# The opening of a chunked linear attention: own terms, diagonals and masks of two units by halves of heads, four head copies on another engine, and a later place for the loads of v

## Chip, cores and metric

The kernel runs on one core of one Trainium2 chip. The metric is the device time of one execution in microseconds (us). The engines are named as in the profile: PE is TensorE (matmuls, with PEld for its weight loads), DVE is VectorE, ACT is ScalarE, POOL is GpSimd, and SP is the queue that issues most DMA loads.

## What is computed

The reference chains two blocks. The first is a linear attention with a decaying state: 4 batches, 8 heads, 768 positions, 48 numbers a head.

```python
for t in range(S):
    kt, vt, rt = (k[:, :, t], v[:, :, t], r[:, :, t])
    cur = np.einsum('bhd,bhe->bhde', u[None] * kt, vt)
    y[:, :, t] = np.einsum('bhd,bhde->bhe', rt, state + cur)
    state = w[None, :, :, None] * state + np.einsum('bhd,bhe->bhde', kt, vt)
```

So a position sees its own key and value through `u` (the own term), and all earlier ones through powers of the decay `w`. The second block takes the 3072 rows of y (384 wide), scores them against 8 experts, gives each expert its 384 rows in the order of the scores, and runs each expert's two matrices (384 to 1024, a ReLU, 1024 to 384) over its rows. The change touches only the start of the first block.

## The kernel before

The attention is cut into 24 units, each 128 positions of one batch (`units`: for each of the 6 chunks in time, the 4 batches). For a unit, k and r are turned (heads in pairs, transposed on PE), and each is scaled by a table of powers of w, so that one matmul per head, `pairs`, gives all products of a key with a later position. Entries on and below the diagonal of that 128 x 128 square are not wanted. The diagonal is to hold the own term r·(u k). This is put together so:

- `own` (L439) multiplies r by k and by u on POOL, two instructions of 384 columns into `rk`. `own_sum` (L446) sums it over the 48 numbers of each head on DVE into `dd` (8 numbers a row).
- `diagonal` (L487) makes, for each of the 8 heads, a 128 x 128 square with `dd` on its diagonal, on ACT (L495), in the tile `AT`.
- `pairs` (L497) runs 16 matmul instructions into `g_ps` (L504), and then copies the products over `AT` where a mask allows it, in two DVE instructions (L508), one for each z, the place of a head in its pair.
- `outputs` (L531) multiplies v by `AT` on PE (L542), and ACT copies the result out (`x`, L560). `rows` turns it back (`x_ps`, L591), ACT copies it (`xr`, L598), and SP stores it.
- `keep` adds the unit to its batch's state, from keys scaled on POOL (`keys`, L433, tile `kss`, with the table `wk`).

There is one more step: eight heads are laid out so that the pairs need one head twice. `again_one` (L342) copies that head's 48 columns on ACT, once for k and once for r; the last of the four transposes of a unit's k or r reads the copy, and so does `keys`.

The decay tables come from `start` (L346): powers of w are formed on DVE in steps (`powers`, L378 to L387), then their reciprocal (L393), and two outer products `Q` (L395), one on POOL and one on DVE. ACT copies pieces of `Q` into the tables `WK` and `WR` (`table`, L420); unit 0 is scaled by the pieces of `Q` itself. `wk_turned` and `wk_table` give `wk` from `WK`, through PE. `spread_u` brings u to all 128 partitions with a matmul, and `copy_u` (L412) copies it to `u_bc` on ACT. `idle` (L415) issues transposes whose result nobody reads.

The order of the work is written out by hand: under `manual_schedule` each engine executes its instructions in the order in which `run` (L613) issues them. `run` opens with units 0 and 1 and the sums and diagonals for both, then loops over the units; iteration n turns unit n + 2, makes its diagonals, runs the pairs of unit n + 1, and finishes unit n. In the opening, unit 2's sum stands before unit 1's pairs and masks (L659 to L664). SP issues the loads in the order written at L357, and then three in each iteration: k and r of unit n + 5 and v of unit n + 4. There are 5 buffers for k and r, 6 for v, so k of unit 5 needs every reader of k of unit 0 to be done. The tiles `g_ps` and `y_ps` have one buffer each.

Of the kernel before, what the change touches and what calls it, by code (L numbers as in the profile page):

```python
# [10 lines left out]
F32 = mybir.dt.float32  # L11
# [5 lines left out]
ALU = mybir.AluOpType  # L17
AX = mybir.AxisListType
# [3 lines left out]
T = 128  # L22
# [252 lines left out]
class Mild:  # L275
# [65 lines left out]

    def again_one(self, n, x):  # L342
        t, HP, H, D = self.krs[:, n % self.NK, x], self.HP, self.H, self.D
        self.nc.scalar.copy(t[:, H, 0:D], t[:, HP, 0:D])

    def start(self):  # L346
# [3 lines left out]
        with nc.allow_non_contiguous_dma(reason="a row to the partitions"):  # L350
            for eng, z, aa, hh in ((nc.sync, 0, slice(0, half), slice(0, HP, 2)),
# [4 lines left out]
                eng.dma_start(self.wp[z * PD:z * PD + D, aa], self.w[hh].rearrange("h d -> d h"))  # L356
        for n, what in ((0, "kr"), (1, "kr"), (0, "v"), (2, "kr"), (1, "v"), (3, "kr"), (2, "v"), (4, "kr"), (3, "v")):  # L357
            self.load(n, what)
# [34 lines left out]
        nc.vector.reciprocal(AB[:, 1], AB[:, 0])  # L393
        for x, eng in ((0, nc.gpsimd), (1, nc.vector)):
            eng.tensor_mul(self.Q[:, x], AB[:, x, :, 1, :].unsqueeze(3).to_broadcast([128, HP, 9, 8]),  # L395
                           AB[:, x, :, 0, 0:8].unsqueeze(2).to_broadcast([128, HP, 9, 8]))
        Q = self.Q.rearrange("p x a i j -> p x a (i j)")
# [40 lines left out]

    def own(self, n):  # L439
        nc, H, D = self.nc, self.H, self.D  # L440
        rk = self.pool.tile([128, H, D], F32, name="rk")
        nc.gpsimd.tensor_mul(rk, self.krs[:, n % self.NK, 1, 0:H, 0:D], self.krs[:, n % self.NK, 0, 0:H, 0:D])  # L442
        nc.gpsimd.tensor_mul(rk, rk, self.u_bc)  # L443
        self.live[n].update(rk=rk)

    def own_sum(self, n):  # L446
        dd = self.pool.tile([128, self.H], F32, name="dd")
        self.nc.vector.tensor_reduce(out=dd, in_=self.live[n]["rk"], axis=AX.X, op=ALU.add)  # L448
        self.live[n]["dd"] = dd

# [35 lines left out]

    def diagonal(self, n, zs=(0, 1)):  # L487
        nc, HP = self.nc, self.HP
        if "AT" not in self.live[n]:
            self.live[n]["AT"] = self.pool.tile([128, 2, HP, T], F32, name="AT", bufs=3)  # L490
        AT, dd = self.live[n]["AT"], self.live[n]["dd"]
        for z in zs:
            for a in range(HP):
                h = self.head(a, z)
                nc.scalar.mul(AT[:, z, a, :], self.ident, dd[:, h:h + 1])  # L495

    def pairs(self, n, between=None):  # L497
        nc, HP, D = self.nc, self.HP, self.D
        kT, rT, AT = (self.live[n][x] for x in ("kT", "rT", "AT"))
        g_ps = self.ps.tile([128, 2, HP, T], F32, name="g_ps")  # L500
        for a in range(HP):
            for z in range(2):
                rows = slice(z * PD, z * PD + D)
                nc.tensor.matmul(g_ps[:, z, a, :], kT[rows, a, :], rT[rows, a, :], start=True, stop=True)  # L504
        if between is not None:
            between()
        for z in range(2):
            nc.vector.copy_predicated(out=AT[:, z], mask=self.mask.unsqueeze(1).to_broadcast([128, HP, T]),  # L508
                                      data=g_ps[:, z])

    def keep(self, n):
# [101 lines left out]
    def run(self, step):  # L613
        N, B, C, walk = self.N, self.B, self.C, self.walk
        self.live = {n: {} for n in range(N)}
        self.start()
        u_ps = self.spread_u()
        self.again_one(0, 0)
        k0 = self.keys_turned(0, True)
        self.again_one(0, 1)  # L620
        self.idle(2, "g_ps")
        r0 = self.r_turned(0)
        self.copy_u(u_ps)
        self.own(0)
        self.scaled(0, "k", k0, "pieces")
        self.scaled(0, "r", r0, "pieces")
        self.table(self.WK, "k")
        self.again_one(1, 0)
        self.table(self.WR, "r")
        self.again_one(1, 1)  # L630
        self.idle(2, "g_ps")
        k1 = self.keys_turned(1, True, walk.ps, "few")
        wk_ps = self.wk_turned()
        r1 = self.r_turned(1, walk.ps, "counts")
        self.wk_table(wk_ps)
        self.scaled(1, "k", k1, self.WK)
        self.own_sum(0)
        self.diagonal(0, (0,))
        self.again_one(2, 0)
        self.diagonal(0, (1,))  # L640
        self.again_one(2, 1)
        self.scaled(1, "r", r1, self.WR)
        self.own(1)
        self.keys(0)
        self.own_sum(1)
        nc, AB = self.nc, self.ones8
        nc.vector.tensor_mul(self.chunk, AB[:, 0, :, 1, 8], AB[:, 0, :, 1, 8])
        self.pairs(0)
        self.diagonal(1)
        self.own(2)  # L650
        chores = walk.constants()
        for n in range(N):
            self.load(n + 5, "kr")
            self.load(n + 4, "v")
            if n == 2:
# [3 lines left out]
            if n == 0:  # L659
                self.turn(2, True)  # L660
                self.own_sum(2)
                self.idle(3, "y_ps")
                self.pairs(1)
                self.keys(1)  # L664
# [1212 lines left out]
```

## Time and profile before

| | |
|---|---|
| median of 3 runs | 398.21 us (397.88 to 398.33) |
| the profiled execution | 398.63 us |
| its span, first to last instruction | 396.9 us |
| granted TensorE clock | 0.996 |
| PE busy in the span | 381.1 us (96%) |
| DVE | 267.4 us (67%) |
| ACT | 161.3 us (41%) |
| POOL | 137.9 us (35%) |
| the chain of work that ended last | PE 73%, DVE 10%, ACT 3%, POOL 3%, DMA 3% |

The span runs from the first to the last instruction of the profiled execution; its time holds 1.7 us more around it. Times of single instructions below are counted from the start of the span. The median comes from other executions of the same kernel. The attention with its gate fills the first 100 us or so, and the experts the rest. A row of a timeline gives the start, the duration (of a group: from its start to its end), the engine, the line, what is written and read, and how often; an idle time ahead of it is in brackets with what ended it. Neighbouring instructions on an engine overlap by some 0.1 us at their ends, so a sum over many of them is made from start to next start.

### The profile page before, as it was taken

Reading aid. Unit: us, or ns where it says so; the run is one execution under the profiler, and the core shown is the slowest. Engines: PE = TensorE matmul, PEld = TensorE weight load, DVE = VectorE, ACT = ScalarE, POOL = GpSimd, SP = SyncE. Lnnn points to the kernel's source line nnn. Section 1 sums busy time; section 2 is a strip of 40 time slices with the busy share of each in tenths; the row PEclk is TensorE's granted clock in tenths of the full one; section 3 lists DMA queues with packets and bytes.
Section 4 is the critical chain, followed back from the end, with each engine's and each line's share of the span. In section 5 each row is a group of like instructions: output and inputs, shape, how many; then the busy total and the mean of one; then the engine's idle time right before and its main releaser. Section 6 shows DMA issues by size and latency. Waiting matters only on the chain.

```text
span 396.9 us, 8692 instructions
## 1 busy us (share of the span) xinstructions
PE 381.1 (96%) x3243; PEld 289.4 (73%) x3243; DVE 267.4 (67%) x934; ACT 161.3 (41%) x429; POOL 137.9 (35%) x173
## 2 busy tenths in 40 slices
PE   7899999999999998999999999999999999999993
PEld 5678888888877764587578569558757857966981
DVE  6755777576885787967839819979578663952620
ACT  4997878888873311222222122221222222222220
POOL 7888877666732022031121120302303221040020
PEclk9999999999999999999999999999999999999998
DMA  9999999897692164641460650109209173370010
GB/s 121 158 184 205 197 201 171 151 177 153 125 327 81 42 247 169 215 164 40 152 246 12 220 208 2 60 0 334 84 21 359 57 281 120 99 300 2 2 61 26
DMA packets 95331, 57.29 MB, mean 144 GB/s; under 512 B 77232, under 2 KB 89520, under 8 KB 95280
## 3 DMA queue, kind: packets, MB, share of 16 engines
q1 hardware_dynamic: 91936, 47.21, 47.4%
q0 software_dynamic: 3104, 9.44, 6.7%
q8 instruction: 27, 0.44, 0.5%
q14 instruction: 24, 0.20, 0.2%
q10 hardware_dynamic: 240, 0.00, 0.0%
HBM read 47.20 MB, written 9.44 MB: 143 GB/s over the span
## 4 chain that ended last, share of the span: by engine, by line
PE 73%; DVE 10%; issue 4%; ACT 3%; POOL 3%; DMA 3%; SPq 1%; POOLq 0%; another core or an unknown queue 0%; DVEq 0%; ACTq 0%
PE h_ps L1539 26%; PE p_ps L1614 14%; PE o_ps L1641 7%; PE y_ps L542 6%; PE g_ps L504 4%; PE e_h_ps L1709 3%; PE kv_ps L521 2%; DMA krs<-in_k_dram 2%; PE kT_ps L458 2%; ACT AT L495 2%; PE x_ps L591 2%; PE lg_ps L571 2%; PE xT_ps L1526 2%; DVE W L1591 2%; PE rT_ps L458 1%
## 5 line engine op out<-in xcount | busy, mean ns | idle before, releaser
L1539 PE MATMUL h_ps<-xT,w 128*128 128x384 f32 (+1 forms) x384 | 120.8, 467 | 0.6 <-ACT e_o_sb L1721 0.6
L1539 PEld LDWEIGHTS h_ps<-xT,w 128*128 128x128 f32 x384 | 66.7, 190 | 39.1 <-issue 2.2
L1541 ACT ACTIVATE hid<-h_ps 128x384 f32<-128x384 f32 (+1 forms) x64 | 29.7, 464 | 91.3 <-PE h_ps L1539 79.9
L495 ACT ACTIVATE AT<-ident,dd 128x128 f32<-128x128 f32 x192 | 59.1, 391 | 2.0 <-DVE dd L448 1.8
L1511 POOL DMA_INDIRECT xg<-x_rows,tok x22 | 21.9, 997 | 88.0 <-issue 36.0
L1635 POOL DMA_INDIRECT out_dram<-o_all,to x16 | 17.6, 1103 | 99.2 <-DVE o_all L1623 66.8
L508 DVE COPY_PREDICATED AT<-mask,g_ps 128x512 f32<-128x512 uint8 x48 | 32.6, 732 | 12.1 <-PE g_ps L504 10.7
L1618 ACT COPY res<-p_ps 128x384 f32<-128x384 f32 (+2 forms) x28 | 13.2, 473 | 60.5 <-PE p_ps L1614 58.4
L1641 PE MATMUL o_ps<-w,hid 128*128 128x384 f32 x96 | 33.1, 488 | 0.0
L504 PE MATMUL g_ps<-rT,kT 48*128 48x128 f32 x384 | 27.9, 284 | 0.7 <-DVE AT L508 0.6
L436 POOL TENSOR_TENSOR kss<-krs,wk 128x384 f32<-128x384 f32 x24 | 24.3, 1017 | 8.0 <-DVE krs L340 5.5
L504 PEld LDWEIGHTS g_ps<-rT,kT 48*128 48x128 f32 x384 | 23.4, 187 | 4.0 <-PE unread_ps L418 0.5
L542 PE MATMUL y_ps<-AT,vts 128*64 128x128 f32 x384 | 25.7, 276 | 0.0
L443 POOL TENSOR_TENSOR rk<-rk,u_bc 128x384 f32<-128x384 f32 x24 | 24.2, 1007 | 1.9
L442 POOL TENSOR_TENSOR rk<-krs 128x384 f32<-128x384 f32 x24 | 24.6, 1024 | 0.2 <-DMA krs<-in_r_dram 0.2
L1641 PEld LDWEIGHTS o_ps<-w,hid 128*128 128x128 f32 x96 | 17.2, 190 | 9.5 <-issue 0.2
L542 PEld LDWEIGHTS y_ps<-AT,vts 128*64 128x64 f32 x384 | 20.6, 137 | 1.2 <-issue 0.7
L1614 PE MATMUL p_ps<-T,S 128*128 128x192 f32 x120 | 20.9, 328 | 0.0
L1591 DVE TENSOR_TENSOR H<-hid 128x512 f32<-128x512 f32 x12 | 7.9, 687 | 19.1 <-ACT hid L1541 19.1
L560 ACT COPY x<-y_ps 128x512 f32<-128x512 f32 x24 | 14.0, 585 | 14.6 <-PE y_ps L542 14.6
L1614 PEld LDWEIGHTS p_ps<-T,S 128*128 128x128 f32 x120 | 19.6, 190 | 0.1
L1614 PE MATMUL p_ps<-w,hid 128*128 128x192 f32 (+1 forms) x112 | 19.0, 316 | 0.0
(303 smaller groups left out, 684.9 us busy)
## 6 DMA issues: line engine op xcount, KB each, us to landing
w<-in_moe_w_dram SPq DMA_DIRECT2D x18, 1536.0 KB, 6.8
krs<-in_k_dram SPq DMA_DIRECT2D x24, 192.0 KB, 4.4
krs<-in_r_dram SPq DMA_DIRECT2D x24, 192.0 KB, 4.9
vts<-in_v_dram SPq DMA_DIRECT2D x24, 192.0 KB
x_rows<-xr SPq DMA_DIRECT2D x24, 192.0 KB, 3.0
xg<-x_rows,tok POOLq DMA_INDIRECT x22, 4.2
out_dram<-o_all,to POOLq DMA_INDIRECT x16, 2.7
out_dram<-o_sb,to POOLq DMA_INDIRECT x5
```

Source lines behind the costliest of these rows:

```text
L436: self.nc.gpsimd.tensor_mul(self.kss[:, n % self.NS].rearrange("p (g h) d -> p g h d", g=2)[:, :, :, 0:D], src, self.wk.rearrange("p (g h) ...
L442: nc.gpsimd.tensor_mul(rk, self.krs[:, n % self.NK, 1, 0:H, 0:D], self.krs[:, n % self.NK, 0, 0:H, 0:D])
L443: nc.gpsimd.tensor_mul(rk, rk, self.u_bc)
L495: nc.scalar.mul(AT[:, z, a, :], self.ident, dd[:, h:h + 1])
L504: nc.tensor.matmul(g_ps[:, z, a, :], kT[rows, a, :], rT[rows, a, :], start=True, stop=True)
L508: nc.vector.copy_predicated(out=AT[:, z], mask=self.mask.unsqueeze(1).to_broadcast([128, HP, T]), data=g_ps[:, z])
L542: nc.tensor.matmul(yv[q * PD:(q + 1) * PD, o // 2, o % 2, :], lhsT, rhs, start=(o // 2, q) not in seen, stop=stop, skip_group_check=True)
L1511: nc.gpsimd.indirect_dma_start(out=xg[:, c, :], out_offset=None, in_=x_dram[0:within, :], in_offset=bass.IndirectOffsetOnAxis(ap=tok[:, c: ...
L1539: nc.tensor.matmul(h_ps[:, 0:m], w1[:, f, ts(j, 128)], xT[:, f, 0:m], start=(f == 0), stop=(f == KD - 1))
L1541: nc.scalar.activation(hid[:, j, 0:m], h_ps[:, 0:m], AF.Relu)
L1614: nc.tensor.matmul(ps[:, q, :], left[a][:, j, :], right[b][:, j, :], start=(j == 0), stop=(j == KF // 2 - 1))
L1641: nc.tensor.matmul(o_ps, hid[:, j, ts(c, 128)], w2[:, j, :], start=(j == 0), stop=(j == KF - 1))
```

## The change

In `start`, both products `Q` are formed on DVE. The loads are reordered: v of each unit stands after k and r of a later unit, and the loop loads v of unit n + 3 instead of n + 4. The head copies of units 1 and 2 go from ACT to POOL. For units 0 and 1, `own` does its second product in two halves of heads, `own_sum` sums each half, `diagonal` makes each half, and the masks are two instructions by halves of the pairs, each over both z (`masked_half`), instead of one for each z. For unit 0, `own` begins with k times u. The order in `run` is new; in iteration 0, unit 2's sum now follows unit 1's pairs and masks.

```diff
--- before.py
+++ after.py
@@ -339,9 +339,9 @@
         kr, HP, H, D = self.krs[:, n % self.NK], self.HP, self.H, self.D
         self.nc.vector.tensor_copy(kr[:, :, H, 0:D], kr[:, :, HP, 0:D])
 
-    def again_one(self, n, x):
+    def again_one(self, n, x, copy=None):
         t, HP, H, D = self.krs[:, n % self.NK, x], self.HP, self.H, self.D
-        self.nc.scalar.copy(t[:, H, 0:D], t[:, HP, 0:D])
+        (copy or self.nc.scalar.copy)(t[:, H, 0:D], t[:, HP, 0:D])
 
     def start(self):
         nc, HP, H, D = self.nc, self.HP, self.H, self.D
@@ -354,7 +354,7 @@
                                    (nc.scalar, 1, slice(half, HP - 1), slice(HP + 2, HP + 3)),
                                    (nc.scalar, 1, slice(HP - 1, HP), slice(HP, HP + 1))):
                 eng.dma_start(self.wp[z * PD:z * PD + D, aa], self.w[hh].rearrange("h d -> d h"))
-        for n, what in ((0, "kr"), (1, "kr"), (0, "v"), (2, "kr"), (1, "v"), (3, "kr"), (2, "v"), (4, "kr"), (3, "v")):
+        for n, what in ((0, "kr"), (1, "kr"), (2, "kr"), (0, "v"), (3, "kr"), (1, "v"), (4, "kr"), (2, "v")):
             self.load(n, what)
         make_identity(nc, self.ident)
         nc.vector.memset(self.krs[:, :, :, :, D:PD], 0.0)
@@ -391,9 +391,9 @@
         for i in range(2):
             powers(i)
         nc.vector.reciprocal(AB[:, 1], AB[:, 0])
-        for x, eng in ((0, nc.gpsimd), (1, nc.vector)):
-            eng.tensor_mul(self.Q[:, x], AB[:, x, :, 1, :].unsqueeze(3).to_broadcast([128, HP, 9, 8]),
-                           AB[:, x, :, 0, 0:8].unsqueeze(2).to_broadcast([128, HP, 9, 8]))
+        for x in range(2):
+            nc.vector.tensor_mul(self.Q[:, x], AB[:, x, :, 1, :].unsqueeze(3).to_broadcast([128, HP, 9, 8]),
+                                 AB[:, x, :, 0, 0:8].unsqueeze(2).to_broadcast([128, HP, 9, 8]))
         Q = self.Q.rearrange("p x a i j -> p x a (i j)")
         M = PD
         self.pieces = {"k": ((slice(0, M + 1), Q[:, 0, :, M::-1]), (slice(M + 1, T), Q[:, 1, :, 1:T - M])),
@@ -436,17 +436,27 @@
         self.nc.gpsimd.tensor_mul(self.kss[:, n % self.NS].rearrange("p (g h) d -> p g h d", g=2)[:, :, :, 0:D], src,
                                   self.wk.rearrange("p (g h) d -> p g h d", g=2))
 
-    def own(self, n):
+    def own(self, n, u_first=False):
         nc, H, D = self.nc, self.H, self.D
+        k, r = (self.krs[:, n % self.NK, x, 0:H, 0:D] for x in range(2))
         rk = self.pool.tile([128, H, D], F32, name="rk")
-        nc.gpsimd.tensor_mul(rk, self.krs[:, n % self.NK, 1, 0:H, 0:D], self.krs[:, n % self.NK, 0, 0:H, 0:D])
-        nc.gpsimd.tensor_mul(rk, rk, self.u_bc)
+        if u_first:
+            nc.gpsimd.tensor_mul(rk, k, self.u_bc)
+        else:
+            nc.gpsimd.tensor_mul(rk, r, k)
+        for hs in self.parts(n):
+            nc.gpsimd.tensor_mul(rk[:, hs], rk[:, hs], r[:, hs] if u_first else self.u_bc[:, hs])
         self.live[n].update(rk=rk)
 
-    def own_sum(self, n):
-        dd = self.pool.tile([128, self.H], F32, name="dd")
-        self.nc.vector.tensor_reduce(out=dd, in_=self.live[n]["rk"], axis=AX.X, op=ALU.add)
-        self.live[n]["dd"] = dd
+    def parts(self, n):
+        H = self.H
+        return (slice(0, H // 2), slice(H // 2, H)) if n < 2 else (slice(0, H),)
+
+    def own_sum(self, n, part=0):
+        if "dd" not in self.live[n]:
+            self.live[n]["dd"] = self.pool.tile([128, self.H], F32, name="dd")
+        hs = self.parts(n)[part]
+        self.nc.vector.tensor_reduce(out=self.live[n]["dd"][:, hs], in_=self.live[n]["rk"][:, hs], axis=AX.X, op=ALU.add)
 
     def pair(self, t, a):
         s = 2 * a if t.shape[1] == self.H or 2 * a < self.HP else 2 * a + 1
@@ -484,7 +494,7 @@
         self.scaled(n, "k", kT_ps, self.WK if raw else None)
         self.scaled(n, "r", rT_ps, self.WR)
 
-    def diagonal(self, n, zs=(0, 1)):
+    def diagonal(self, n, zs=(0, 1), hs=range(99)):
         nc, HP = self.nc, self.HP
         if "AT" not in self.live[n]:
             self.live[n]["AT"] = self.pool.tile([128, 2, HP, T], F32, name="AT", bufs=3)
@@ -492,7 +502,8 @@
         for z in zs:
             for a in range(HP):
                 h = self.head(a, z)
-                nc.scalar.mul(AT[:, z, a, :], self.ident, dd[:, h:h + 1])
+                if h in hs:
+                    nc.scalar.mul(AT[:, z, a, :], self.ident, dd[:, h:h + 1])
 
     def pairs(self, n, between=None):
         nc, HP, D = self.nc, self.HP, self.D
@@ -504,9 +515,16 @@
                 nc.tensor.matmul(g_ps[:, z, a, :], kT[rows, a, :], rT[rows, a, :], start=True, stop=True)
         if between is not None:
             between()
-        for z in range(2):
+        for z in range(2) if n > 1 else ():
             nc.vector.copy_predicated(out=AT[:, z], mask=self.mask.unsqueeze(1).to_broadcast([128, HP, T]),
                                       data=g_ps[:, z])
+        return g_ps
+
+    def masked_half(self, n, g_ps, i):
+        half = self.HP // 2
+        at = slice(i * half, (i + 1) * half)
+        mask = self.mask.unsqueeze(1).unsqueeze(1).to_broadcast([128, 2, half, T])
+        self.nc.vector.copy_predicated(out=self.live[n]["AT"][:, :, at], mask=mask, data=g_ps[:, :, at])
 
     def keep(self, n):
         nc, HP, D, C = self.nc, self.HP, self.D, self.C
@@ -614,53 +632,61 @@
         N, B, C, walk = self.N, self.B, self.C, self.walk
         self.live = {n: {} for n in range(N)}
         self.start()
+        first, second = range(self.H // 2), range(self.H // 2, self.H)
+        nc, AB = self.nc, self.ones8
         u_ps = self.spread_u()
         self.again_one(0, 0)
         k0 = self.keys_turned(0, True)
+        self.copy_u(u_ps)
+        self.own(0, True)
         self.again_one(0, 1)
         self.idle(2, "g_ps")
         r0 = self.r_turned(0)
-        self.copy_u(u_ps)
-        self.own(0)
+        self.own_sum(0, 0)
         self.scaled(0, "k", k0, "pieces")
+        self.own_sum(0, 1)
         self.scaled(0, "r", r0, "pieces")
         self.table(self.WK, "k")
-        self.again_one(1, 0)
+        self.diagonal(0, hs=first)
         self.table(self.WR, "r")
-        self.again_one(1, 1)
-        self.idle(2, "g_ps")
+        self.diagonal(0, hs=second)
+        for x in range(2):
+            self.again_one(1, x, nc.gpsimd.tensor_copy)
+        self.idle(3, "g_ps")
         k1 = self.keys_turned(1, True, walk.ps, "few")
+        r1 = self.r_turned(1, walk.ps, "counts")
+        self.scaled(1, "k", k1, self.WK)
+        self.own(1)
+        self.scaled(1, "r", r1, self.WR)
+        g0 = self.pairs(0)
         wk_ps = self.wk_turned()
-        r1 = self.r_turned(1, walk.ps, "counts")
         self.wk_table(wk_ps)
-        self.scaled(1, "k", k1, self.WK)
-        self.own_sum(0)
-        self.diagonal(0, (0,))
-        self.again_one(2, 0)
-        self.diagonal(0, (1,))
-        self.again_one(2, 1)
-        self.scaled(1, "r", r1, self.WR)
-        self.own(1)
+        self.masked_half(0, g0, 0)
+        self.own_sum(1, 0)
+        self.diagonal(1, hs=first)
+        self.masked_half(0, g0, 1)
+        self.own_sum(1, 1)
+        self.diagonal(1, hs=second)
+        for x in range(2):
+            self.again_one(2, x, nc.gpsimd.tensor_copy)
         self.keys(0)
-        self.own_sum(1)
-        nc, AB = self.nc, self.ones8
+        self.own(2)
         nc.vector.tensor_mul(self.chunk, AB[:, 0, :, 1, 8], AB[:, 0, :, 1, 8])
-        self.pairs(0)
-        self.diagonal(1)
-        self.own(2)
         chores = walk.constants()
         for n in range(N):
             self.load(n + 5, "kr")
-            self.load(n + 4, "v")
+            self.load(n + 3, "v")
             if n == 2:
                 self.gate_weights()
             soon, split = n <= B, 0 < n < 3
             halves = ((0,), (1,)) if split else ((0, 1), ())
             if n == 0:
                 self.turn(2, True)
+                self.idle(3, "y_ps")
+                g1 = self.pairs(1)
+                for i in range(2):
+                    self.masked_half(1, g1, i)
                 self.own_sum(2)
-                self.idle(3, "y_ps")
-                self.pairs(1)
                 self.keys(1)
             else:
                 step(n, "first")
```

## The prediction

> **What bounds the kernel now.** I read the list of cores first (one core, 396.9 us, clock 0.996, so no clock effect), then the chain of waits over the first 70 us, then each engine's timeline from 4 to 31 us. The busy table by stage (columns: us, then PE, PEld, DVE, ACT, POOL busy with instruction counts, clock, DMA share, GB/s) shows where the opening ends:
>
> ```profile
> 10.00:15.00 5.00, 3.45 (x41) 2.61 (x39) 4.12 (x8) 4.97 (x18) 4.65 (x6) 1.00 1.51 163
> 20.00:25.00 5.00, 4.29 (x66) 3.73 (x62) 2.26 (x5) 5.00 (x17) 4.90 (x6) 1.00 1.27 178
> 25.00:30.00 5.00, 4.83 (x65) 4.10 (x66) 3.52 (x7) 5.00 (x18) 3.99 (x5) 1.00 1.14 194
> 40.00:50.00 10.00, 10.00 (x172) 8.68 (x168) 7.85 (x23) 8.63 (x25) 8.86 (x16) 1.00 1.03 195
> ```
>
> From 40 us TensorE is full; from 10 to 30 us ScalarE (ACT) is, and it paces TensorE. The chain of waits (start, us, what) agrees: VectorE (DVE) work leads to x_ps of unit 0, then it stays on ACT until 30.82, then on PE:
>
> ```profile
> 13.60 0.66 DVE kT L477
> 14.26 0.60 DVE rT L477
> 14.86 0.20 DVE dd L448
> ...
> 15.25 1.36 DVE AT L508 x2
> ...
> 18.92 0.40 PE x_ps L591 x4
> ...
> 19.34 0.48 ACT xr L598
> ...
> 30.23 0.60 ACT x L560
> 30.82 0.05 issue
> 30.87 0.60 PE x_ps L591 x4
> ```
>
> The ACT timeline shows which work this is. The last diagonals before the loop's copies are those of unit 2, from 15.35, just behind their sum dd of unit 2 (DVE 14.79 + 0.53 = 15.32):
>
> ```profile
> 12.70 2.45 ACT L495 ACTIVATE AT<-ident,dd 128x128 f32<-128x128 f32 x8
> 15.06 0.22 ACT L344 COPY krs<-krs 128x48 f32<-128x48 f32 x1
> 15.35 2.45 ACT L495 ACTIVATE AT<-ident,dd 128x128 f32<-128x128 f32 x8
> 17.71 0.21 ACT L344 COPY krs<-krs 128x48 f32<-128x48 f32 x1
> 17.83 0.58 ACT L560 COPY x<-y_ps 128x512 f32<-128x512 f32 x1
> 18.52 0.58 ACT L475 COPY kT<-kT_ps 112x512 f32<-112x512 f32 x1
> 19.34 0.48 ACT L598 COPY xr<-x_ps 128x384 f32<-128x384 f32 x1 [0.24 <-PE x_ps L591]
> ```
>
> From 15.35 to 30.8 ACT has about 0.35 us of gaps (18.41 to 18.52, 19.10 to 19.34). So what the change is worth is **when ACT starts the diagonals of unit 2**. That start carries through almost one to one, since what ACT does after it is unchanged and from 30.87 PE works back to back with its work fixed.
>
> **What the skill says.** (1) "PSUM — Partial Sum Buffer", Engine vs sequencer instructions: the ScalarE, VectorE and GpSimdE queues are strict FIFO. The trace agrees: each engine's rows stand in the order written. (2) "SBUF — State Buffer", Who interferes with whom: a VectorE instruction with two SBUF inputs and a GpSimd instruction that reads SBUF exclude each other, whichever starts second blocking until the first ends. The trace agrees:
>
> ```profile
> 11.39 1.01 POOL L436 TENSOR_TENSOR kss<-krs,wk 128x384 f32<-128x384 f32 x1
> 11.94 0.48 DVE L647 TENSOR_TENSOR chunk<-ones 128x4 f32<-128x4 f32 x1
> ```
>
> Chunk has the size of L384, which took 0.17; it took 0.48 and ended at 12.42, when GpSimd's product ended (12.40). (3) "GPSIMD Engine Reference", Performance versus the Vector engine: elementwise is about 2x slower on GpSimd. Here Q took 0.68 on GpSimd and 0.46 on DVE, 0.38 from its start to the next one's.
>
> **The change, part by part.** DVE steps below are from start to next start; all are from the timelines.
>
> *Copies of head blocks off ACT.* Four copies of L344 (0.23 each, 0.12 of ACT's time where the next follows): 4 x 0.12 = 0.5 us off ACT, before unit 2's diagonals. On GpSimd no such copy was seen: at least the 128x1 memset's 0.10, at most the 128x128 cast's 0.29; I take 0.13. They lie ahead of unit 1's and unit 2's own terms on GpSimd, 0.5 us in all (0.4 to 1.2; no gain, since GpSimd did none before).
>
> *Own term of unit 0, k by u first.* The copy of u on ACT moves ahead of the second head copy: u_ps is done near 5.46, so u is copied 5.5 to 5.97 and the first product runs 6.02 to 7.03, instead of starting at 7.05. Its halves (192 columns, 0.51 by L527) end near 7.66 and 8.13. Work for 0.9 us earlier, but its first product now lies over the powers on DVE. L382 is at 5.94, L387 at 6.14, both SBUF by SBUF. GpSimd gets in between: **L387 blocks from 6.14 to about 7.05, 0.9 us**. Bounds: 0, if the product starts after 6.14, and 1.0, the whole product. I take 0.9 (reciprocal at 7.25 instead of 6.36).
>
> *Q all on DVE.* One Q more, 0.38, on the engine. The first wants to start at 7.88, with GpSimd's second half going until 8.13: it waits 0.25; the second ends its turn at 8.88. Tables and unit 0's scaling wait for that, where before scaling began at 7.37.
>
> *The DVE order to the sum of unit 2.* From 8.88: half sum of unit 0 0.26 (0.46 less 192 columns at about 1 ns), k scaled 0.67, half sum 0.26, r scaled 0.67, unit 1 k 0.63, r 0.63 (before: 0.66), half mask 0.66 (512 elements, as one z of L508), half sum 0.28, half mask 0.66, half sum 0.28, chunk 0.30 (0.12 alone, 0.5 blocked), unit 2 k 0.60, r 0.60, both half masks of unit 1 1.32, then the sum of unit 2, 0.53. Neither half is in the trace: a half sum lies between half of L448's 0.46 and all of it, a half mask between 0.60 and 0.75 (L508 lasts 0.71 to 0.76), so four masks and four sums make −0.4 to +1.1. The list is 8.35, so it ends at 17.23 and unit 2's diagonals start near 17.28. **The sum now stands behind unit 1's masks**, whereas before it stood ahead of them (14.79 against 15.25). This is the one new wait on ACT. Queued behind it are the copies of y, kT and x of the loop; PE waits for these at x_ps.
>
> *What lies beside it.* ACT: Q 8.88, WK to 9.3, half diagonals 1.2, WR 0.7, half 1.2 (to 12.4), wk table after pairs(0) and its transposes near 12.55 to 13.0, unit 1's diagonals in two halves to 15.45, one copy, then idle until 17.28. GpSimd: keys of unit 0 wait for wk (13.05 to 14.05), own term of unit 2 to 16.1, which is 0.6 before DVE reaches its sum (16.7), so it and the four copies are hidden; if that cover is gone they add what passes 0.6. PE: one idle transpose more (0.19) inside the wait for k of unit 1 until 7.66; pairs(0) 10.8 to 11.9, wk's transposes, now behind it, to 12.5; pairs(1) 13.65 to 14.8, outputs of unit 0 to 15.9, all ahead of need.
>
> *Loads.* k and r of units 2 to 4 move up one place in SP's queue, about 1.19 us each (7.17 less 5.98): unit 2's transposes could start at 10.1 instead of 11.29. They feed a VectorE that isn't there before 14.2, so nothing comes of it. v of unit 0 moves two places back: it lands near 12.5 (r of unit 2 landed at 12.48 in that place), before outputs at 14.8. In the loop v is loaded a unit later, with three units of 4.6 us to spare. k of unit 5 must wait for keys of unit 0 (14.05), with r and v behind it on SP; before, it was issued at 18.24, so this is hidden.
>
> *Sum.* Unit 2's diagonals start 17.28 − 15.35 = 1.93 later. Of the gaps behind, 1.51 us from the start of x of unit 0 to xr shrinks to 1.28 (30.23 to 31.51, where nothing else is late): −0.23. Net **+1.7 us**. Against the profiled execution: span 396.9 → 398.6, its time 398.63 → 400.3. That execution lies 0.4 above the median, so on the median 398.2 → **399.9**. What is late next: the DVE chain itself.
>
> **Rivals.** (a) *Order without the block.* The first product starts after 6.14 and blocks no power, only the first Q, until about 7.2: the second Q's turn ends near 7.95 instead of 8.88, diagonals near 16.35, +1.0 − 0.23 = +0.8: 399.0. For it: 0.1 us decides. Against: the u copy is ready at 5.5. (b) *Faster: DVE keeps up.* If the masks by halves, with the pair's port free, cost so much less that the sum of unit 2 ends before 15.3, ACT isn't starved. Its own list from 7.45 (0.7 + 1.2 + 0.7 + 1.2 + 0.45 + 2.4 + 0.1) ends at 14.2, and unit 2's diagonals start up to 1.1 earlier: 397.1. For it: ACT loses 0.5 us of copies and starts unit 0 earlier. Against: 8.35 us of listed DVE work would have to take 6.4. It decides at 15.3. (c) *Nothing reaches the end*: the later search and weight loads set it, 398.2. Against: the chain of waits is PE for 73% with no wait for a DMA after the opening. (d) *More blocks*: own terms and keys block chunk, or GpSimd's copies cost 0.29 and the own term of unit 2 arrives after 16.7; +3: 401.2.
>
> **Chances.** Forecast 0.50, (a) 0.20, (b) 0.12, (c) 0.10, (d) 0.08. A measurement of this kernel can tell about 0.2%, 0.8 us, from no change. Slower by more: the forecast, half of (a), (d): 0.68. Within: (c), half of (a): 0.20. Faster: 0.12. Range 398.3 to 400.8: it takes in (a), leaves out (b), most of (d), and part of (c), about 0.2.
>
> **What would show it.** Right: L387 lasting about 1 us near 6.1; unit 2's sum at about 16.7 behind two 512-element masks; ACT idle for over 1.5 us before its diagonals; PE's gapless work from 32.5 instead of 30.87. Wrong: L387 at 0.18; unit 2's diagonals starting before 15.4; gapless PE before 30.9; or an unchanged end with a late opening.

## The result and the profile after

| | before | changed |
|---|---|---|
| median of 7 runs | 398.23 us (397.88 to 398.46) | 399.56 us (399.43 to 401.1) |
| profiled execution | 398.63 us | 399.56 us |
| its span | 396.9 us | 397.8 us |

The changed kernel takes 1.0040 of the time before (95% interval 1.0031 to 1.0050). The medians lie 1.3 us apart; the ratio goes with the averages, which are 1.6 us apart because two of the changed kernel's runs took 400.1 and 401.1 us.

The chain of waits of the changed kernel's trace holds only its last 15 us, so the opening is read from the timelines. First ScalarE, the same stretch as before the change (start, duration, engine, line, tiles, and in brackets the idle time ahead and what ended it):

```profile
12.71 2.45 ACT L506 ACTIVATE AT<-ident,dd 128x128 f32<-128x128 f32 x8
15.06 0.21 ACT L344 COPY krs<-krs 128x48 f32<-128x48 f32 x1
16.82 2.45 ACT L506 ACTIVATE AT<-ident,dd 128x128 f32<-128x128 f32 x8 [1.54 <-DVE dd L459]
19.17 0.21 ACT L344 COPY krs<-krs 128x48 f32<-128x48 f32 x1
19.29 0.58 ACT L578 COPY x<-y_ps 128x512 f32<-128x512 f32 x1
19.77 0.58 ACT L485 COPY kT<-kT_ps 112x512 f32<-112x512 f32 x1
20.56 0.48 ACT L616 COPY xr<-x_ps 128x384 f32<-128x384 f32 x1 [0.21 <-PE x_ps L609]
```

Unit 1's diagonals start when they did before, within 0.01 us, and ScalarE is free at 15.27. Then it waits 1.54 us for the sum of unit 2, so that unit 2's diagonals start at 16.82 instead of 15.35. Before, its longest wait in this stretch was one of 0.24 us. The VectorE timeline shows why the sum is late:

```profile
6.15 0.17 DVE L387 TENSOR_TENSOR ones<-ones 128x16 f32<-128x16 f32 x1
6.88 1.64 DVE L395 TENSOR_TENSOR Q<-ones 128x288 f32<-128x288 f32 x2
8.44 0.34 DVE L459 TENSOR_REDUCE dd<-rk 128x4 f32<-128x192 f32 x1
...
15.01 1.34 DVE L527 COPY_PREDICATED AT<-mask,g_ps 128x512 f32<-128x512 uint8 x2
16.25 0.54 DVE L459 TENSOR_REDUCE dd<-rk 128x8 f32<-128x384 f32 x1
```

Unit 1's two half masks (15.01) stand ahead of the sum (16.25); before, the sum started at 14.79, ahead of the masks. Earlier, the two Q take 1.64 us. The GpSimd timeline has the products that lie over them:

```profile
6.43 1.00 POOL L444 TENSOR_TENSOR rk<-krs,u_bc 128x384 f32<-128x384 f32 x1 [1.15 <-ACT u_bc L413]
7.51 1.46 POOL L448 TENSOR_TENSOR rk<-rk,krs 128x192 f32<-128x192 f32 x2
```

The delay then moves through PE unchanged. These are the starts of the transposes into x_ps at four places of the two traces (in both, the last of them comes after 128 us, so the attention lasts longer than the 100 us given above):

| x_ps | before | changed | later by |
|---|---|---|---|
| unit 0 | 18.75 | 19.92 | 1.17 |
| unit 3 | 30.87 | 32.08 | 1.21 |
| near 61 us | 61.27 | 62.48 | 1.21 |
| near 122 us | 122.01 | 123.22 | 1.21 |

Behind that 0.3 us is won back at the last matmuls of the gate (lg_ps), which start 0.83 us after x_ps of the unit ahead of them in the trace of before (125.62, 126.45) and 0.53 us after it in the changed one's (126.83, 127.36). Then the delay stays at 0.87 from the experts' first copy of hid at 159 us to about 270 us, and lies between 0.83 and 1.30 behind that. The last part differs from trace to trace (in the third experiment below, the copies of hid are 0.26 us behind before, then 0.44, then 0.8). The timed medians, 1.33 apart, are the better measure of the end.

### The profile page after: what moved, and what is told of

It is laid out like the page before. It is cut to its first block, busy times and chain, and to the rows that moved or that the text cites. A ratio compares the mean times of both kernels' runs of the same rounds, so it can differ in the third digit from the quotient of the medians.

```text
span 397.8 us, 8688 instructions
## 1 busy us (share of the span) xinstructions
PE 382.5 (96%) x3244; PEld 291.0 (73%) x3244; DVE 268.3 (67%) x937; ACT 160.8 (40%) x425; POOL 138.2 (35%) x178
## 5 line engine op out<-in xcount | busy, mean ns | idle before, releaser
L519 DVE COPY_PREDICATED AT<-mask,g_ps 128x512 f32<-128x512 uint8 x44 | 30.0, 733 | 12.5 <-PE g_ps L515 10.6
L448 POOL TENSOR_TENSOR rk<-rk,u_bc 128x384 f32<-128x384 f32 (+1 forms) x24 | 23.3, 972 | 1.8
L446 POOL TENSOR_TENSOR rk<-krs 128x384 f32<-128x384 f32 x23 | 23.2, 1010 | 0.0
```

The lines of the kernel that those rows point to most:

```text
L446: nc.gpsimd.tensor_mul(rk, r, k)
L448: nc.gpsimd.tensor_mul(rk[:, hs], rk[:, hs], r[:, hs] if u_first else self.u_bc[:, hs])
```

## Experiments

Each kernel was timed against the kernel before on its own chip, which there took 398.26 to 399.12 us. Ratios with their 95% intervals are therefore compared, not microseconds. For scale: 1 us is 0.0025. The last two columns come from each kernel's trace. "Theory 1" in the expectations is the explanation held at that point: the later sum on VectorE, the time lost in Q, and the own term of unit 2 on GpSimd all delay the start of unit 2's diagonals, and the end follows that start.

| kernel | ratio to before | unit 2's diagonals | xr of unit 0 |
|---|---|---|---|
| before | 1 | 15.35 | 19.34 |
| changed | 1.0040 (1.0031 to 1.0050) | 16.82 | 20.56 |
| order only | 1.0031 (1.0019 to 1.0043) | 17.22 | 20.96 |
| sum first | 1.0036 (1.0023 to 1.0049) | 16.55 | 20.50 |
| sum and own term first | 1.0012 (1.0004 to 1.0020) | 15.60 | 19.57 |
| Q alone | 1.0038 (1.0020 to 1.0056) | 16.57 | 20.48 |
| write only | 1.0028 (1.0018 to 1.0038) | 16.51 | 20.25 |
| product early | 1.0051 (1.0039 to 1.0063) | 16.88 | 20.62 |
| Q back | 1.0038 (1.0025 to 1.0051) | 17.42 | 21.16 |
| loads back | 1.0032 (1.0020 to 1.0044) | 16.82 | 20.56 |
| copies back | 1.0033 (1.0021 to 1.0045) | 16.85 | 20.59 |
| best parts | 1.0003 (0.9994 to 1.0011) | 15.52 | 19.50 |
| sum early | 0.9993 (0.9985 to 1.0001) | 15.10 | 19.07 |
| sum between | 0.9995 (0.9986 to 1.0003) | 14.70 | 19.19 |

The traces don't all have PE at the same pace in the opening (last section): before, Q alone, write only and sum between have the faster one, the others the slower. At the slower pace, unit 2's diagonals in the kernel before would start near 15.7 instead of 15.35. This is an estimate from the order-only trace, where ScalarE is through with unit 1's diagonals and the head copy behind them at about 15.57 + 0.12. So rows of unlike pace are compared only to some 0.35 us in the last two columns; the ratios do not depend on the traces.

**The order alone**, in the kernel before:

```diff
-                self.own_sum(2)
                 self.idle(3, "y_ps")
                 self.pairs(1)
+                self.own_sum(2)
```

> The kernel before with one edit: in iteration 0 the sum of unit 2 is issued behind unit 1's pairs and masks instead of ahead of them. Theory 1 (the order on VectorE alone is worth most of what the change lost): masks of unit 1 at 14.8, sum at 16.1, unit 2's diagonals near 16.65 instead of 15.35 on ScalarE, idle there for 1.4 us, xr of unit 0 near 20.4 instead of 19.34: slower than before by 1.1 us (0.8 to 1.4). Rival (masks ahead let PE and VectorE run ahead, so the wait is made good by unit 3): within 0.4 us of before.

It was 1.3 us slower. In its trace unit 0's sum and diagonals stand 0.6 us later than in the trace of before, for a reason given in the last section; within its own trace the cost of the order can still be seen, in the DVE timeline and then the ACT timeline:

```profile
14.45 0.69 DVE L477 TENSOR_TENSOR rT<-rT_ps,WR 112x512 f32<-112x512 f32 x1
15.39 1.36 DVE L508 COPY_PREDICATED AT<-mask,g_ps 128x512 f32<-128x512 uint8 x2 [0.25 <-PE g_ps L504]
16.65 0.54 DVE L448 TENSOR_REDUCE dd<-rk 128x8 f32<-128x384 f32 x1
```

```profile
17.22 2.45 ACT L495 ACTIVATE AT<-ident,dd 128x128 f32<-128x128 f32 x8 [1.44 <-DVE dd L448]
```

With the sum in its old place it would have followed the scaling, at about 14.45 + 0.60 = 15.05; it starts at 16.65, 1.6 us later, and ScalarE waits 1.44 us. So the order by itself costs most of what the whole change lost: about three quarters by the ratios (1.0031 of 1.0040), nearly all by the medians (1.30 of 1.33 us). The intervals overlap, so the share isn't known more closely. The rival, that the wait is made good by unit 3, fell.

**The sum first**, in the changed kernel: the same move undone.

```diff
                 self.turn(2, True)
+                self.own_sum(2)
                 self.idle(3, "y_ps")
...
                     self.masked_half(1, g1, i)
-                self.own_sum(2)
```

> The changed kernel with unit 2's sum moved back ahead of unit 1's pairs and masks, nothing else. Theory 1 (three causes close together: the order on VectorE, the time lost in Q, and GpSimd's own term of unit 2, which in the changed kernel ends only 0.3 us before VectorE reaches the sum): the sum now waits for GpSimd until 15.9, unit 2's diagonals start near 16.5 instead of 16.82, and unit 1's masks, now behind the waiting sum, end near 17.8, so xr of unit 0 stays within 0.3 us of 20.56 and the time is 399.3 to 399.7, no gain over the changed kernel. Rival (the order on VectorE alone made the change slow): diagonals of unit 2 at 15.5, xr near 19.5, time 398.3 to 398.5.

The ratio stays that of the changed kernel within the intervals, as theory 1 had it; undoing the order isn't enough. In the DVE timeline the sum now waits for GpSimd instead, and the masks behind it are late (16.43 instead of 15.01):

```profile
15.96 0.55 DVE L459 TENSOR_REDUCE dd<-rk 128x8 f32<-128x384 f32 x1 [0.86 <-POOL rk L448]
16.43 1.33 DVE L527 COPY_PREDICATED AT<-mask,g_ps 128x512 f32<-128x512 uint8 x2
```

**The sum and the own term first**: the same, and on GpSimd

```diff
-        self.keys(0)
         self.own(2)
+        self.keys(0)
```

> As the run before, and on GpSimd the own term of unit 2 stands ahead of the keys of unit 0, which wait for the table wk from ScalarE. Theory 1: the own term ends near 14.0, the sum of unit 2 follows the scaling at 15.0, diagonals of unit 2 start near 15.6, xr of unit 0 near 19.5, time about 1.0 us less than the changed kernel's, 398.3 to 398.7. If the lost time in Q were what the end follows, moving the sum would leave the diagonals of unit 2 past 16.4 and the time above 399.2.

1.0012: some 1.1 us of the 1.6 (1.0040 on 399.0) are back. Unit 2's diagonals start at 15.60 and xr of unit 0 at 19.57, both as expected:

```profile
15.60 2.45 ACT L506 ACTIVATE AT<-ident,dd 128x128 f32<-128x128 f32 x8 [0.31 <-DVE dd L459]
```

The order on GpSimd is not a part of the change: the kernel before has keys of unit 0 ahead of the own term of unit 2 as well. What the change moved is the table wk, which these keys read. Its transposes on PE now stand behind unit 0's pairs, and its copy on ScalarE behind unit 0's diagonals. Two rows of before (the copy, and the second product of the own term), then the changed kernel's:

```profile
8.99 0.47 ACT L431 COPY wk<-wk_ps 128x384 f32<-128x384 f32 x1
13.69 1.00 POOL L443 TENSOR_TENSOR rk<-rk,u_bc 128x384 f32<-128x384 f32 x1
```

```profile
12.29 0.48 ACT L431 COPY wk<-wk_ps 128x384 f32<-128x384 f32 x1 [0.38 <-PE wk_ps L427]
12.85 1.02 POOL L436 TENSOR_TENSOR kss<-krs,wk 128x384 f32<-128x384 f32 x1 [1.04 <-ACT wk L431]
14.91 1.01 POOL L448 TENSOR_TENSOR rk<-rk,u_bc 128x384 f32<-128x384 f32 x1
```

The copy of wk comes 3.3 us later, keys of unit 0 wait for it, and the own term of unit 2 ends at 15.92 instead of 14.69. This run goes round that delay; it doesn't undo it. So two things together hold about 70% of the loss by the ratios: the sum behind the masks, and the late wk ahead of unit 2's own term. With the first undone, the second kept unit 2's diagonals late (the run before). That undoing the second alone would gain nothing is read from the changed kernel's trace, where the own term is done 0.33 us before VectorE reaches the sum; it was not run. What is left, 1.0012, is not taken apart.

**Q alone**, in the kernel before:

```diff
-        for x, eng in ((0, nc.gpsimd), (1, nc.vector)):
+        for x, eng in ((0, nc.vector), (1, nc.vector)):
```

> The kernel before with one edit: both Q are formed on VectorE. Theory 1 (GpSimd, free of its Q, starts r by k when r of unit 0 lands at 6.45, and excludes the two Q in turn): the pair of Q takes 1.6 to 2.3 us from the start of the first to the end of the second, unit 0's scaling starts at 8.5 to 9.2 instead of 7.37, diagonals of unit 0 start 1.0 to 1.7 us later and the time is 0.8 to 1.5 us above before. Rival (VectorE only has one more product of 0.38 to do): Q takes 0.84, scaling starts at 7.75, and the time is within 0.4 us of before.

Its DVE timeline, and then GpSimd's:

```profile
6.88 2.19 DVE L395 TENSOR_TENSOR Q<-ones 128x288 f32<-128x288 f32 x2
8.99 0.74 DVE L473 TENSOR_TENSOR kT<-kT_ps,Q 112x260 f32<-112x260 f32 x2
```

```profile
6.58 1.00 POOL L442 TENSOR_TENSOR rk<-krs 128x384 f32<-128x384 f32 x1 [1.30 <-DMA krs<-in_r_dram]
7.67 1.09 POOL L443 TENSOR_TENSOR rk<-rk,u_bc 128x384 f32<-128x384 f32 x1
```

The pair takes 2.19 us where two alone take 0.76 (next run), each behind one of GpSimd's products; unit 0's diagonals start at 11.49 instead of 10.03 (both traces have the faster pace). The medians are 0.9 us apart, within what was expected; the ratio makes it 1.5 us (0.8 to 2.2). Either of two edits alone, the order or Q, thus costs the kernel before most of what the whole change does. The costs don't add: both delay the same start.

**Write only**: the changed kernel with GpSimd's first product exchanged.

```diff
-            nc.gpsimd.tensor_mul(rk, k, self.u_bc)
+            nc.gpsimd.tensor_copy(rk[:, 0:1, 0:1], self.u_bc[:, 0:1, 0:1])
+            for _ in range(2):
+                nc.gpsimd.memset(rk, 0.01)
```

> The changed kernel with GpSimd's first product of unit 0 (k by u, reading SBUF for 1.0 us) replaced by a one-column copy and two memsets of the same tile, which only write, for about 0.9 us in all; so unit 0's own term leaves out k and u. Theory 1 (a VectorE product with two SBUF inputs and a GpSimd instruction that reads SBUF exclude each other): the two Q take about 0.8 us from the start of the first instead of 1.64, less what GpSimd's half products still block; the first half sum starts at 7.8 to 8.1 instead of 8.44, unit 2's diagonals 0.3 to 0.6 us earlier, time 399.0 to 399.3. Rival (the Q last long for another reason, such as their own shape or the reciprocal they read): Q takes 1.5 us or more and the time stays at 399.5.

GpSimd, and then DVE:

```profile
6.23 0.89 POOL L446 MEMSET rk<- 128x384 f32 x2
```

```profile
6.88 0.76 DVE L395 TENSOR_TENSOR Q<-ones 128x288 f32<-128x288 f32 x2
8.12 0.35 DVE L461 TENSOR_REDUCE dd<-rk 128x4 f32<-128x192 f32 x1 [0.48 <-POOL rk L450]
```

GpSimd is busy until 7.1, 0.24 us past the start of Q, and yet the two Q now take 0.76 instead of 1.64. So it is not a busy GpSimd that holds up Q, but one whose product reads SBUF. Of the 0.88 us only 0.31 reaches unit 2's diagonals, because the half sum then waits for GpSimd's half product. By the ratios the time is 0.5 us lower, which these intervals don't separate from the changed kernel.

**Product early**: the changed kernel with k by k in place of k by u.

```diff
-            nc.gpsimd.tensor_mul(rk, k, self.u_bc)
+            nc.gpsimd.tensor_mul(rk, k, k)
```

> The changed kernel with GpSimd's first product of unit 0 made k by k, so that it waits for no u and starts when k lands, near 5.35; so unit 0's own term leaves out u. This puts it over VectorE's powers, as the prediction had it. Theory 1 (exclusion): one of the powers that follow lasts until about 6.35 and the reciprocal starts 0.6 to 1.1 us later than 6.36; GpSimd's halves then meet the last powers or the first Q; the first half sum starts at 8.4 to 9.2 instead of 8.44, and the time is 0 to 0.8 us above the changed kernel. Rival (products of so few elements are not held up): reciprocal at 6.36, Q met by the halves alone, first half sum at 7.7 to 8.1, time 0.3 to 0.7 us below the changed kernel.

GpSimd, and then DVE:

```profile
5.40 0.82 POOL L444 TENSOR_TENSOR rk<-krs 128x384 f32<-128x384 f32 x1
```

```profile
5.54 0.70 DVE L384 TENSOR_TENSOR ones<-ones 128x4 f32<-128x4 f32 x1
```

This is the block of the prediction, made to happen. A product of 4 columns that takes 0.17 alone took 0.70 and ended at 6.24, when GpSimd's ended (6.22). The reciprocal came 0.53 later (6.89), a little under the 0.6 expected at least, since this product took 0.82 and not 1.00; the two Q then took 1.16, and the first half sum started at 8.50. The trace is thus only 0.06 behind the changed kernel's, the time perhaps 0.4, and the intervals overlap.

**Q back** on GpSimd, in the changed kernel:

```diff
-        for x in range(2):
-            nc.vector.tensor_mul(self.Q[:, x], ...
+        for x, eng in ((0, nc.gpsimd), (1, nc.vector)):
+            eng.tensor_mul(self.Q[:, x], ...
```

> The changed kernel with the first Q back on GpSimd. Theory 1: GpSimd's own term of unit 0 then starts after its Q, near 7.1, and its first half ends near 8.9, so VectorE, which has the half sum ahead of unit 0's scaling, waits for it until 8.9 to 9.1 instead of starting it at 8.44: unit 2's diagonals 0.3 to 0.7 us later than 16.82, and the time 1.6 to 2.1 us above before, that is 0.3 to 0.7 above the changed kernel. Rival (Q on VectorE is what made the change slow): 0.4 to 0.9 us below the changed kernel.

VectorE waits 1.58 us for the half product and starts the half sum at 9.03:

```profile
9.03 0.35 DVE L459 TENSOR_REDUCE dd<-rk 128x4 f32<-128x192 f32 x1 [1.58 <-POOL rk L448]
```

Unit 2's diagonals come at 17.42, 0.60 after the changed kernel's. In time (+1.5 us) it isn't told apart from the changed kernel, and it falls just short of what I expected; the gain that the rival expected isn't there. By the trace, once the half sum stands ahead of unit 0's scaling, forming Q on VectorE was the lesser evil.

**Loads back** and **copies back**, two parts of the changed kernel undone:

```diff
-        for n, what in ((0, "kr"), (1, "kr"), (2, "kr"), (0, "v"), (3, "kr"), (1, "v"), (4, "kr"), (2, "v")):
+        for n, what in ((0, "kr"), (1, "kr"), (0, "v"), (2, "kr"), (1, "v"), (3, "kr"), (2, "v"), (4, "kr"), (3, "v")):
...
-            self.load(n + 3, "v")
+            self.load(n + 4, "v")
```

> The changed kernel with the order of loads as before (v of unit 0 ahead of k and r of unit 2, v of unit n + 4 in the loop). Theory 1: k of unit 2 lands 1.2 us later, near 11.3, and r near 12.5, where PE wants them at 12.1 and 12.5 and GpSimd's copy of r at 11.6; keys of unit 0 wait for wk until 12.85 anyway. No change, 399.3 to 399.8. Rival (the order of loads, not the order on the engines, holds up the opening or a later v): a change of over 0.5 us either way.

```diff
         self.table(self.WK, "k")
+        self.again_one(1, 0)
+        self.again_one(1, 1)
         self.diagonal(0, hs=first)
...
-        for x in range(2):
-            self.again_one(1, x, nc.gpsimd.tensor_copy)
...
+        self.again_one(2, 0)
+        self.again_one(2, 1)
         self.wk_table(wk_ps)
...
-        for x in range(2):
-            self.again_one(2, x, nc.gpsimd.tensor_copy)
```

> The changed kernel with the four head copies of units 1 and 2 back on ScalarE, ahead of unit 0's diagonals and of the table wk. Theory 1 (ScalarE waits 0.4 us before wk and 1.5 us before unit 2's diagonals, and GpSimd waits for wk): 0.5 us of copies on ScalarE and 0.8 us less on GpSimd both fall into waits: unit 2's diagonals within 0.3 us of 16.82, time within 0.3 us of the changed kernel, 1.0 to 1.7 above before. Rival (the copies on GpSimd hold up unit 1's own term and so the chain): 0.4 to 0.8 us below the changed kernel.

Both give the changed kernel's opening to 0.03 us (16.82 and 16.85), and times that are the same within the intervals. By the medians (+1.03 and +0.86 us) they lie about 0.1 us below my ranges, by the ratios (+1.3 us both) inside them. In the traces neither part does anything here: what they free ends in waits.

**Best parts**: the kernel before with the new loads, head copies of unit 2 on GpSimd, and these moves.

```diff
         self.own(1)
+        for x in range(2):
+            self.again_one(2, x, self.nc.gpsimd.tensor_copy)
+        self.own(2)
         self.keys(0)
...
                 self.pairs(1)
+                nc.vector.tensor_mul(self.chunk, AB[:, 0, :, 1, 8], AB[:, 0, :, 1, 8])
```

> The kernel before with the parts of the change that theory 1 holds to be sound and its order on VectorE: loads in the new order, head copies of unit 2 on GpSimd behind unit 1's own term, own term of unit 2 ahead of the keys of unit 0, and chunk moved behind unit 1's masks so that no GpSimd product holds it up ahead of unit 0's. Theory 1: unit 0's diagonals end at 12.4 instead of 12.6, the sum of unit 2 starts near 14.45, its diagonals near 15.0 instead of 15.35, xr of unit 0 near 18.95 instead of 19.34: 0.2 to 0.5 us below before. Rival (the kernel before is bound by ScalarE's own list from the first diagonals on, or PE's chain through pairs(2) is late next): within 0.2 us of before.

No difference from before is seen; of the gain I expected, 0.2 to 0.5 us, the interval leaves room for 0.2. The ACT timeline:

```profile
10.24 0.48 ACT L431 COPY wk<-wk_ps 128x384 f32<-128x384 f32 x1 [1.11 <-PE wk_ps L427]
10.64 4.79 ACT L495 ACTIVATE AT<-ident,dd 128x128 f32<-128x128 f32 x16
```

All 16 diagonals of units 0 and 1 run without a gap from 10.64 to 15.43, so from the first diagonal on ScalarE's own list sets unit 2's start, as the rival had it. The first one came late because ScalarE waited 1.11 us for PE, which had the slower pace here; so this trace doesn't say what the moves are worth at the faster one.

**Sum early**: that version, with unit 0's second product and sum by halves and ahead of unit 1's scaling, and wk behind unit 0's diagonals.

```diff
+        self.own_sum(0, 0)
+        self.diagonal(0, hs=range(self.H // 2))
+        self.own_sum(0, 1)
+        self.diagonal(0, hs=range(self.H // 2, self.H))
         self.wk_table(wk_ps)
         self.scaled(1, "k", k1, self.WK)
-        self.own_sum(0)
-        self.diagonal(0)
```

> The version with the best parts (new loads, head copies of unit 2 on GpSimd, own term of unit 2 ahead of the keys of unit 0, chunk moved back), and further: unit 0's second own product and its sum by halves, both half sums ahead of unit 1's scaling on VectorE, and the table wk behind unit 0's diagonals on ScalarE. Theory 1, as that run left it (from the first diagonal on ScalarE works through its own list without a gap, so only an earlier first diagonal helps): the first half sum ends near 9.25, unit 0's diagonals start near 9.3 instead of 10.03 before and 10.64 in that run, unit 2's near 15.0, set by VectorE again, xr of unit 0 near 19.0: 0.2 to 0.7 us below before. Rival (the chain through VectorE's masks and pairs(2) on PE is equally late): within 0.2 us of before.

Unit 0's diagonals start at 9.41, unit 2's at 15.10, xr of unit 0 at 19.07. The ratio, 0.9993, agrees with a gain of 0.3 us but also with none.

**Sum between**: one more move, unit 2's sum between its two scalings.

```diff
-                self.turn(2, True)
+                k2, r2 = self.keys_turned(2, True), self.r_turned(2)
+                self.scaled(2, "k", k2, self.WK)
                 self.own_sum(2)
+                self.scaled(2, "r", r2, self.WR)
```

> The last version (half sums of unit 0 early) with one more move: the sum of unit 2 between the scaling of its k and of its r on VectorE, where its own term on GpSimd (done near 14.0) just allows it. Unit 1's masks start no later, since the same three instructions stand ahead of them. Theory 1: unit 2's diagonals start near 14.7, right behind unit 1's and a head copy, instead of 15.10, and xr of unit 0 near 18.8 instead of 19.07; time 0.4 to 0.8 us below before, so 0.1 to 0.4 below the last version. Rival (PE's chain through pairs(2) and the turning of unit 3 is late by then): no change against the last version, 0.1 to 0.4 below before.

ScalarE's timeline, behind the copy of x of unit 0 (17.17):

```profile
18.37 0.58 ACT L481 COPY kT<-kT_ps 112x512 f32<-112x512 f32 x1 [0.63 <-PE kT_ps L464]
```

and PE's, ahead of that:

```profile
16.59 1.16 PE L511 MATMUL g_ps<-rT,kT 48*128 48x128 f32 x16 [0.36 <-DVE AT L515]
17.68 0.65 PE L464 MATMUL kT_ps<-ident,kss 128*112 128x128 f32 x4
```

Unit 2's diagonals start where they should, at 14.70, and the gain is lost at once: ScalarE waits 0.63 us for the turned keys of unit 3, which PE reaches only after the pairs of unit 2 (16.59), which wait for unit 1's masks on VectorE. Here the rival was right, and theory 1, that the start of unit 2's diagonals decides, ends: by these traces it holds down to about 15 us, where a second chain is equally late. In time, sum early and sum between aren't told apart from before or from each other.

## Why the prediction was right, and where it was off

The forecast was +1.7 us; it came to +1.33 by the medians, inside the range. By its steps:

- **What bounds the opening: right.** The start of unit 2's diagonals moved by 1.47 us, xr of unit 0 by 1.22, and PE's gapless work by 1.21. The forecast for the gap that shrinks behind (−0.23) came out at −0.25. About 0.35 of the 1.47, by the estimate under the table, may be the slower pace of PE in the later trace and not the change. Of the delay at x_ps, 0.3 us was made good at lg_ps, which the forecast did not have.
- **The sum behind the masks: right.** From the first half sum to the start of unit 2's sum the list had 7.82 us; it took 16.25 − 8.44 = 7.81. That it agrees to the hundredth is luck: a wait of about 0.2 us for unit 0's pairs, which the list did not have, was made up by masks and half sums that were 0.2 us shorter together. The order-only run shows that this order alone costs some 1.3 us.
- **The block at L387: wrong, and it is the step that was mis-sized.** L387 took 0.17 and the reciprocal started at 6.36. The copy of u ended at 6.35, not 5.97, because PE was at its slower pace in this execution and u_ps was only read at 5.87 (the forecast took 5.5 from the trace of before, where PE had the faster pace); so the product started at 6.43, past the powers, as rival (a) assumed. It met Q instead: 0.88 us lost there (1.64 less 0.76). The forecast had 0.9 for the power and 0.25 for Q; one block took place, not two, and the first half sum started at 8.44 instead of 8.88. That 0.44 is nearly all of the difference between 17.28 and 16.82. Rival (a) had the right place and too small a price, since it let only the first Q wait. In write only, at the faster pace, u was copied by 5.93 and GpSimd started at 5.99, so there the forecast's start would have been met; no trace shows the changed kernel itself at that pace.
- **GpSimd's cover of 0.6 us: half of it there.** The own term of unit 2 ended at 15.92, 0.33 before VectorE reached the sum. The run with the sum first showed what that means: when the sum moves up, the own term, which the late wk holds back, becomes the wait. The forecast had wk this late and took it as hidden.
- **Copies, loads: right at nothing**, by the two runs that undo them.
- **Rival (b)**, VectorE keeping up, fell: half masks took 0.63 and half sums 0.26 from start to start, about as listed (0.66 and 0.28). **(c)** fell: the delay reached the end. **(d)** fell.

What stays open is how often PE is at the slower pace in the opening among the timed runs, of either kernel; what the place of wk alone costs; and whether the half masks, sums and diagonals do anything, since no run undoes them alone.

## What to carry to other kernels

When an instruction is moved back in an in-order queue, follow who waits for its result, not only what now runs earlier: the masks came out 0.25 us sooner (16.35 against 16.60), and the sum behind them kept another engine idle for 1.5 us. When undoing a suspected cause changes nothing, look for the next one that is late by almost as much, and relieve both; here, in the changed kernel, the order on VectorE showed its price only once GpSimd's own term no longer stood behind the late wk. Before moving a product with two SBUF inputs to VectorE, see what GpSimd reads at that time.

## What the hardware showed beyond that

PE runs its first 10 us or so at either of two paces. The same step, turning k of unit 0, in the PE timeline of before and then of the changed kernel:

```profile
5.39 0.65 PE L458 MATMUL kT_ps<-ident,krs 128*112 128x128 f32 x4
```

```profile
5.76 1.10 PE L468 MATMUL kT_ps<-ident,krs 128*112 128x128 f32 x4
```

From one transposition to the next this is 0.12 us in the first and 0.22 in the second. The order-only run issues what before does up to that point, and its trace shows 1.10 too, so it is the execution and not the change. Four traces (before, write only, Q alone, sum between) have the faster pace by 5.4 us, the other ten only from a point between 9.2 and 11 us, and two of these (order only, sum early) show the slower pace once more between 11.3 and 13.5. The Trainium skill, "TensorE: Matmul & The Clock Gate", Part 1: The HAM clock gate, says that the array runs at half rate until it has been busy for a window of about 3.4 us, and that the window runs free, so that the point of change depends on where in it the work begins. The ratio of the two paces agrees with that, and so does the fact that the point of change varies between executions. The length does not: in the changed kernel's trace PE has work without a marked wait from 1.44 us on, so that two such windows would be over by 8.3 (an estimate from the page's figure), and the transpositions from 8.58 on still begin at the slower pace. The profile's column of the granted clock shows 1.00 in both cases. In the order of before, the slower pace moves unit 0's diagonals from 10.03 to 10.61; in the changed order it moves the copy of u, as told above.

Smaller things: a GpSimd product in two halves of 192 columns takes 1.15 us from start to end where the whole takes 1.00. A head copy takes 0.19 us on GpSimd and 0.12 of ScalarE's time. And chunk, a product of 4 columns, takes 0.15 us where it falls between two GpSimd products (Q alone, best parts) and 0.40 to 0.69 in the other traces, where it starts beside one.
